# Two 640x640 weight transposes moved from TensorE and piecewise DMA to whole DMA transposes, with exact 128-feature fold chunks, in a gated linear-attention plus GeGLU kernel

## The chip, the cores and the metric

The kernel runs on one core of one Trainium2 chip. The metric is the device time of one execution in microseconds (us). Each kernel was run several times; the medians below are over its runs. Beside the device time, a run reports a *span*: the stretch from the first to the last recorded instruction. The span is some 2 us shorter than the time. The kernel before took 306.58 us (306.54 to 307.19 in four runs).

Names of engines in profile lines: PE is TensorE's matmul side, PEld its weight loads, DVE VectorE, ACT ScalarE, POOL GpSimd, and SPq the sequencer that issues the transfers.

## The reference, cut to what matters

```python
# S = 2048 tokens, D = 640, H = 32 heads of Dh = 20, F = 1728, all bf16
g = sigmoid((x * gate_w).sum(-1, keepdims=True))
q, k, v = split_heads(x @ wqkv)                      # wqkv: 640 x 1920, columns q | k | v
pq = einsum("bhsd,hdf->bhsf", q, w_phi)              # w_phi: one 20x20 matrix per head
pk = einsum("bhsd,hdf->bhsf", k, w_phi)
phi_q = concat([softmax(pq), softmax(-pq)]); phi_k = concat([softmax(pk), softmax(-pk)])
kv = phi_k^T v ;  z = sum_s phi_k                    # per head
o  = (phi_q kv) / (phi_q z + 1e-6)
a  = o @ wo
b  = (gelu(x @ w_gate) * (x @ w_up)) @ w_down
out = g * a + (1 - g) * b
```

Both kernels *fold* w_phi into the projections: x @ Wk @ blockdiag(w_phi) = x @ (Wk @ blockdiag(w_phi)). A fold is a matmul whose stationary operand is a piece of Wk with features on the partitions, that is, Wk *transposed*. So the front of the kernel needs Wk^T and Wq^T (640x640 each), and x^T (features on partitions) for every projection.

## The kernel before: the parts that matter

Everything goes through a helper that waits for the events a buffer needs, then issues. Transfers on the SP queue take 16 semaphore lanes in turn; at the end the SP sequencer waits for each lane and each engine.

```python
def dma(self, qkey, fn, reads=(), writes=(), guard=()):
    q = self.queues[qkey]
    lane = q["rr"]; q["rr"] = (lane + 1) % len(q["lanes"])      # 16 lanes on SP
    ...
def finish(self, eng):
    for q in self.queues.values():
        for L in q["lanes"]:
            if L["count"] > 0: eng.wait_ge(L["sem"], L["count"])
    for e in self.engs.values(): ...                             # then the four engines
```

The loads. k and v come plain, k is transposed on PE later, q is transposed by six DMAs of 640 rows x 128 columns, each starting at a group of six (or four) heads. The transpose of x block 1 is held until the last k/v load has landed, and everything behind it in the queue with it.

```python
xload(0); kvload(0); xload(2)
for kt in range(1, KD): kvload(kt)                    # five loads of 320 KB: k and v
xblock(1, [("wk", KD - 1)])                           # held until the last k/v load landed
for g, (h0, nh) in enumerate(self.GH):                # GH: head groups of 6, 6, 4, 6, 6, 4
    dma_start_transpose(self.wqT[:, g, :], self.wqkv[:, h0*DH : h0*DH + P])
xblock(2); xblock(3)
# ... then the FFN weights
```

PE's front, in order of issue (a fold is six matmuls of 120 or 80 columns):

```python
warm(7); xt(0); xt(1); warm(2)                        # xt: PE transposes of the first x block
vs(0,0); gate_column(3); vs(1,0); xt(2); xt(3)        # vs(t, kt): one step of x_t @ Wv
...                                                   # the rest of vs, the block diagonal
tk(0, 6, "d"); tk(1, 7, "a"); vs(0, 4); ... tk(5, 1, "d")   # 30 PE transposes of k, six copies
fold(0, "k"); fold(1, "k"); v_early(4); fold(2, "k"); ks(0,0); ...; fold(4, "k"); ...
fold(0, "q"); fold(1, "q"); k_early(1); fold(2, "q"); fold(3, "q"); k_early(2); fold(4, "q")
k_early(3); pq(0,1); pq(0,0); pq(0,3); gram(0); pq(0,2)     # pq: an "Eq group", 5 matmuls, 2 exponentials on ACT
```

After that comes a loop over the sixteen token tiles (projection, exponentials, normalisation, Gram matrix) and the FFN. None of it is touched by the change.

The softmax here doesn't subtract the row's maximum and nothing guards it: scores larger than these inputs give would overflow.

## Time and profile before

| | before |
|---|---|
| device time, median | 306.58 us |
| span of the profiled run | 304.5 us |
| PE busy | 296.6 us (97%) |
| first k fold starts | 14.50 us |
| first q fold that waited for DMA | 22.71 us |
| first Eq group starts | 28.23 us |
| third Eq group starts | 30.67 us |

The top of the profile page and its chain summary (share of the span by engine):

```profile
span 304.5 us, 5031 instructions
...
PE 296.6 (97%) x2002; PEld 175.0 (57%) x2028; DVE 162.3 (53%) x317; ACT 105.2 (35%) x186; POOL 30.0 (10%) x61
...
PE 90%; SPq 4%; DMA 3%; ACT 1%; issue 1%; DVE 0%; DVEq 0%; ACTq 0%
```

PE is busy for 97% and is 90% of the chain that ended last; after 50 us its only listed wait is one of 0.2 us.

The list of PE's waits over the whole run (who waited for whom: us in total, times, longest):

```profile
PE ps L532 <- DVE one L528: 1.3, 1, 1.3
PE ps L351 <- DMA wqT<-in_A_wqkv_dram: 0.8, 1, 0.8
PE ps L388 <- DVE w_49 L364: 0.4, 1, 0.4
PE ps L503 <- ACT Eq L509: 0.3, 1, 0.3
...
```

Line 351 is the fold. The first wait is the unavoidable start.

The chain of waits of the first 31 us, in order of time (start, duration, what):

```profile
3.71 5.80 DMA w_49<-in_A_wqkv_dram
...
9.54 2.68 SPq L228
...
12.26 1.26 SPq L233
...
19.28 3.39 DMA wqT<-in_A_wqkv_dram
...
22.71 0.50 PE ps L351 x7
...
24.58 0.58 PE ps L351 x12
...
26.52 0.29 PE ps L351 x6
```

Read it downwards: the k/v loads land at 9.5 us, only then is x block 1 issued (L228), then the q pieces one after another (L233, the first of six shown), and the q folds (L351) start when the last has landed.

The PE timeline shows the folds (start, duration, line and operation, count, idle before):

```profile
11.74 0.72 PE L322 MATMUL ps<-ident,w_49 128*120 128x128 bf16 x10
...
14.50 0.69 PE L351 MATMUL ps<-BD,wkT 120*128 120x120 bf16 x5
...
26.36 0.45 PE L351 MATMUL ps<-BD,wqT 120*128 120x120 bf16 x6
26.65 1.53 PE L371 MATMUL ps<-w_49,xT 128*128 128x384 bf16 x10
28.23 2.10 PE L503 MATMUL ps<-xT,wq_50 128*128 128x512 bf16 x9
30.67 1.25 PE L503 MATMUL ps<-xT,wq_50 128*128 128x512 bf16 x5 [0.34 <-ACT Eq L509]
```

L322 are the PE transposes of k.

### The profile page before, as it was taken

The page shows a single profiled execution, that of the slowest core. Times are in us where ns is not written, and L with a number is a line of the kernel's source. Part 1 is how long each engine was busy: PE and PEld are TensorE (multiplying, and loading weights), DVE is VectorE, ACT ScalarE, POOL GpSimd, SP SyncE. Part 2 cuts the span into 40 slices and gives each one's busy share as a digit, 9 for nine tenths or more (in the row PEclk, how much of TensorE's full clock was granted, in tenths as well). Part 3 has the DMA queues.
Part 4 walks back from the last instruction along what each step waited for, and adds up shares of the span by engine and source line. Part 5 has one row for each costly group of instructions (what it writes and reads, how often), then busy time and mean ns, then how long its engine had stood idle before and what let it go on. Part 6 is the DMA issues. An engine that isn't in the chain of part 4 may idle for free.

```text
span 304.5 us, 5031 instructions
## 1 busy us (share of the span) xinstructions
PE 296.6 (97%) x2002; PEld 175.0 (57%) x2028; DVE 162.3 (53%) x317; ACT 105.2 (35%) x186; POOL 30.0 (10%) x61
## 2 busy tenths in 40 slices
PE   8989999999999999999999999999999999999996
PEld 3656565655555555777545567754457765545763
DVE  1438999986775877234367710435770044567000
ACT  3356776667673222111322211123221122222111
POOL 7200000000000011111011000101110010111000
PEclk9999999999999999999999999999999999999999
DMA  7679994000000011120110111011001001110101
GB/s 242 176 123 248 368 366 156 2 0 0 2 0 2 0 23 25 22 65 23 44 24 0 22 24 43 24 43 23 18 6 43 24 25 43 22 22 2 43 24 43
DMA packets 33043, 18.29 MB, mean 60 GB/s; under 512 B 25147, under 2 KB 32124, under 8 KB 33020
## 3 DMA queue, kind: packets, MB, share of 16 engines
q1 hardware_dynamic: 32368, 17.95, 21.6%
q8 instruction: 16, 0.26, 0.4%
q10 hardware_dynamic: 652, 0.03, 0.1%
q14 instruction: 7, 0.06, 0.1%
HBM read 9.78 MB, written 2.62 MB: 41 GB/s over the span
## 4 chain that ended last, share of the span: by engine, by line
PE 90%; SPq 4%; DMA 3%; ACT 1%; issue 1%; DVE 0%; DVEq 0%; ACTq 0%
PE ps L630 36%; PE ps L712 20%; PE ps L371 11%; PE ps L718 7%; PE ps L503 6%; PE ps L667 4%; PE ps L477 4%; SPq L233 2%; DMA w_49<-in_A_wqkv_dram 2%; PE ps L640 1%; DMA wqT<-in_A_wqkv_dram 1%; SPq L228 1%; SPq L218 1%; ACT Eq L509 1%; PE ps L351 0%
## 5 line engine op out<-in xcount | busy, mean ns | idle before, releaser
L630 PE MATMUL ps<-xT,wu_sb 128*128 128x512 bf16 x253 | 64.2, 379 | 0.8 <-ACT Eq L509 0.2
L712 PE MATMUL ps<-wd_sb,hT 128*128 128x320 bf16 (+2 forms) x447 | 63.5, 299 | 0.1
L630 PE MATMUL ps<-xT,wg_sb 128*128 128x512 bf16 x252 | 63.0, 379 | 0.2
L633 ACT ACTIVATE gl<-ps 128x512 bf16<-128x512 f32 x52 | 31.0, 597 | 83.3 <-PE ps L630 74.2
L635 DVE TENSOR_TENSOR hT<-ps,gl 128x512 bf16<-128x512 f32 x52 | 35.7, 688 | 42.9 <-PE ps L630 42.9
L712 PEld LDWEIGHTS ps<-wd_sb,hT 128*128 128x128 bf16 x448 | 43.1, 98 | 18.2 <-DVE hT L635 0.4
L630 PEld LDWEIGHTS ps<-xT,wu_sb 128*128 128x128 bf16 x260 | 25.4, 98 | 31.1 <-issue 0.7
L630 PEld LDWEIGHTS ps<-xT,wg_sb 128*128 128x128 bf16 x260 | 24.9, 98 | 26.9
L371 PE MATMUL ps<-w_49,xT 128*128 128x512 bf16 (+3 forms) x216 | 39.0, 328 | 0.2
L696 POOL TENSOR_TENSOR Og<-O_57,O_58 128x640 bf16<-128x640 bf16 x16 | 22.3, 1393 | 167.9 <-DVE O_58 L694 167.9
L728 ACT ACTIVATE outsb<-ps,Gm 128x640 bf16<-128x640 f32 (+2 forms) x17 | 13.0, 762 | 74.1 <-PE ps L718 74.1
L371 PEld LDWEIGHTS ps<-w_49,xT 128*128 128x128 bf16 x220 | 20.8, 97 | 18.2
L683 DVE RECIPROCAL RH<-ps 128x32 f32<-128x32 f32 x16 | 5.7, 358 | 43.9 <-PE ps L667 42.8
L449 DVE TENSOR_REDUCE Dk<-Ek 128x64 f32<-128x1280 bf16 x16 | 23.7, 1482 | 7.4 <-ACT gcol L441 7.4
L458 DVE TENSOR_TENSOR Ek<-Ek,Dk 128x640 bf16<-128x640 bf16 x32 | 25.0, 822 | 0.6
L718 PE MATMUL ps<-wo_sb,goT 128*128 128x320 bf16 (+2 forms) x160 | 24.5, 299 | 0.0
L503 PE MATMUL ps<-xT,wq_50 128*128 128x512 bf16 x94 | 23.4, 378 | 0.7 <-ACT Eq L509 0.3
L509 ACT ACTIVATE Eq<-ps 128x512 bf16<-128x512 f32 x40 | 21.8, 607 | 5.8 <-PE ps L503 5.8
L438 ACT ACTIVATE Ek<-ps 128x640 bf16<-128x640 f32 x32 | 20.7, 704 | 4.1 <-PE ps L371 3.1
L718 PEld LDWEIGHTS ps<-wo_sb,goT 128*128 128x128 bf16 x160 | 15.5, 98 | 6.3
L667 PEld LDWEIGHTS ps<-KV,Eq 128*128 128x128 bf16 x192 | 12.0, 98 | 3.1
L667 PE MATMUL ps<-KV,Eq 128*128 128x154 bf16 x192 | 13.7, 221 | 0.0
(73 smaller groups left out, 183.2 us busy)
## 6 DMA issues: line engine op xcount, KB each, us to landing
out_dram<-outsb SPq DMA_DIRECT2D x15, 160.0 KB, 1.8
wd_sb<-in_B_w_down_dram SPq DMA_DIRECT2D x1, 2080.0 KB, 12.6
w_49<-in_A_wqkv_dram SPq DMA_DIRECT2D x5, 320.0 KB, 5.2
wg_sb<-in_B_w_gate_dram SPq DMA_DIRECT2D x1, 1120.0 KB, 6.5
wu_sb<-in_B_w_up_dram SPq DMA_DIRECT2D x1, 1120.0 KB, 9.0
wg_sb<-in_B_w_gate_dram SPq DMA_DIRECT2D x1, 960.0 KB, 8.9
wu_sb<-in_B_w_up_dram SPq DMA_DIRECT2D x1, 960.0 KB, 9.3
wo_sb<-in_A_wo_dram SPq DMA_DIRECT2D x1, 800.0 KB, 10.3
```

The costliest lines, as they stand in the source:

```text
L371: sc.op("pe", lambda e, kt=kt: e.matmul(self.bank(bank)[:, bcol:bcol + n], self.xT[:, kt, t * P:(t + 1) * P], self.w3[:, kt, self.D + c0:s ...
L449: sc.op("dve", lambda e: e.tensor_reduce(self.Dk[:, se, 0, :].rearrange("p (s h) -> p s h", h=H), self.Ek[:, se, :, :].rearrange("p s (h d ...
L458: sc.op("dve", lambda e, v=v, r=r: e.tensor_tensor(v, v, r, ALU.mult), reads=[("Rk", se)], writes=[("Ek", se, s)])
L503: sc.op("pe", lambda e, kt=kt: e.matmul(self.bank(bank), self.wq2[:, kt, i * P:(i + 1) * P], self.xT[:, kt, b * self.BT:(b + 1) * self.BT] ...
L509: sc.op("act", lambda e, s=s, scale=scale: e.activation(self.Eq[:, s, i, b * self.BT:(b + 1) * self.BT], self.bank(bank), AF.Exp, scale=sc ...
L630: sc.op("pe", lambda e, kt=kt, w=w, bk=bk: e.matmul(self.bank(bk), w[:, kt, c * P:(c + 1) * P], xs(kt), start=(kt == 0), stop=(kt == self. ...
L633: sc.op("act", lambda e: e.activation(self.gl[:, slot, :], self.bank(banks[0]), AF.Gelu_apprx_tanh), reads=[("ps", banks[0])], writes=[("g ...
L635: sc.op("dve", lambda e: e.tensor_tensor(self.hT[:, c, :], self.bank(banks[1]), self.gl[:, slot, :], ALU.mult), reads=[("ps", banks[1]), ( ...
L667: sc.op("pe", lambda e, s=s, i=i, n=n, o0=o0, k0=k0, bk=bk, r=r: e.matmul(self.bank(bk)[:, o0:o0 + n], self.Eq[:, s, i, t * P:(t + 1) * P] ...
L696: sc.op("pool", lambda e: e.tensor_tensor(self.Og[:, sl, :], self.O1[:, sl, :], self.O2[:, sl, :], ALU.add), reads=[("O", 0, sl), ("O", 1, ...
L712: sc.op("pe", lambda e: e.matmul(self.bank(bk, w), self.hT[:, c, tt * P:(tt + 1) * P], self.wd_sb[:, c, w0:w0 + w], start=(c == 0), stop=F ...
L718: sc.op("pe", lambda e: e.matmul(self.bank(bk, w), self.goT[:, gs, k, :], self.wo_sb[:, k, w0:w0 + w], start=False, stop=(k == self.KD - 1 ...
```

## The change

Its intent: take the k transposes off PE, take the six q pieces and the held x block off the critical DMA queue, and load x of the first block ahead of the weights. Wk^T and Wq^T each come in one 640x640 DMA transpose. Then their chunks are exact 128-feature chunks, in which heads (20 features) straddle the edges; so the block diagonal is built per chunk with a mask, and folds accumulate overlapping columns in PSUM (six matmuls of 140 or 80 columns instead of 120 or 80).

```diff
@@ loads @@
-        xload(0)
-        kvload(0)
-        xload(2)
-        for kt in range(1, KD):
-            kvload(kt)                     # k and v, 320 KB each
-        xblock(1, [("wk", KD - 1)])
-        for g, (h0, nh) in enumerate(self.GH):
-            sc.dma("sp", ... dma_start_transpose(self.wqT[:, g, :], self.wqkv[:, h0 * DH:h0 * DH + P]) ...)
+        xload(0)
+        xload(2)
+        for kt in range(KD):
+            vload(kt)                      # v alone, 160 KB each
+        def wload(T, c0, key):
+            sc.dma("sp", lambda e: e.dma_start_transpose(T[:, :, :], self.wqkv[:, c0:c0 + D]), writes=[key])
+        wload(self.wkT, D, "wkT")
+        xblock(1)
+        wload(self.wqT, 0, "wqT")
         xblock(2)
         xblock(3)
@@ fold: six matmuls, chunk i of 128 features, heads HLO[i]..HHI[i] @@
+        for i in range(self.KD):
+            lo, hi = self.HLO[i], self.HHI[i]
+            for h in (0, 1):                       # PSUM bank of heads 0-15, 16-31
+                a, z = max(lo, 16 * h), min(hi, 16 * h + 15)
+                ...
+                matmul(bank[:, c0:c0 + n], wT[:, i, kt * P:(kt + 1) * P], self.BD[:, i, k0:k0 + n], start=first, ...)
@@ PE's front @@
-        (two filler matmuls, 30 transposes of k and their copies, k_step(0, kt) between the k folds)
+        f(0, "k", (6, 7), "d")                     # "d": cast on DVE, "a": on ACT
+        f(1, "k", (0, 1), "a")
+        self.v_early(4, 2)
+        f(2, "k", (4, 5), "d")
+        f(3, "k", (6, 7), "d")
+        self.v_early(5, 0)
+        f(4, "k", (4, 5), "d")
+        self.k_early(0, 2)
+        f(0, "q", (6, 7), "d")
+        f(1, "q", (4, 5), "d")
+        self.k_early(1, 0)
+        f(2, "q", (6, 7), "d")
+        f(3, "q", (4, 5), "d")
+        self.k_norm(0)
+        self.k_early(2, 2)
+        f(4, "q", (6, 7), "a")                     # the last cast, now on ACT
+        self.k_norm(1)
+        self.k_early(3, 0)
         self.pq(0, 1, 1)
         self.pq(0, 0, 0)
         self.pq(0, 3, 3)
```

(cut: the order of the x transposes and of the first steps of V, half of V's copies out of PSUM moved from ACT to DVE, the per-chunk block diagonal with the gate column in its second bank, the mask built earlier on POOL, buffer sizes, and keys of the bookkeeping.)

## The prediction

> What bounds the kernel. TensorE: the page has PE busy 296.6 of 304.5 us (97%), and the chain of waits is 90% PE. After 50 us the list of waits shows no PE idle over 0.2 us, so only removing PE work, or PE's gaps in the first 30 us, can pay. The 5 us windows show PE idle 1.3 us in 0–5 (waiting for x), 0.3 in 15–20 and 1.2 in 20–25; "busy" stretches at 14.5–16.1 also hide fold waits. In the chain the 20–25 gap is DMA: x block 1's transpose waits for all five k/v loads (last lands at 9.5 us, a 5.4 us wait of the SP queue), six transposed q pieces then cost 1.27 us of issue each, and the q folds wait for the last until 22.7.
>
> What the change removes.
> - 30 PE transposes of k (timeline: 10 in 0.72, 5 in 0.44; about 65 ns each): about 1.95 us of PE, plus their six copies (0.49 each on DVE, 0.70 on ACT).
> - Two filler matmuls (0.59 us of PE, mostly in a gap that exists anyway).
> - Half of the early plain load: 819 KB of v instead of 1,638 KB of k and v.
> - Fold waits for those copies (about 0.6 us at 14.5–16), the q wait (0.8 us at 22.7), and about 0.5 us before the last k step at 21.2.
>
> What it adds.
> - Two whole 640x640 DMA transposes. Estimate from x blocks (512x640: issue 2.7–2.9 us, landing 4.9–6.6 us after issue, peak near 290 GB/s): issue 3.3 us, data 3 us. The Trainium skill, "DMA: Bandwidth & Descriptors", section "Latency and other measured facts", gives 261 GB/s for non-contiguous and 350–400 for contiguous transposes; this trace's peak lies between. So k^T should land near 10–11 us, x block 1 near 13, q^T near 16, each before its use (12.5, 13.5 and 19).
> - Five block-diagonal matmuls and multiplies instead of two and three: about 0.1 us of PE.
> - A fold stays six matmuls, 720 columns instead of 640. Six took 0.45 us though columns alone need 0.27, so it is weight-load bound: +0.0–0.05 us each.
> - x of both halves before V: V starts at about 6.0 us and runs without gaps for 5.75 us (20 steps of 0.287); folds start at about 12.4 us rather than 14.5.
>
> On the critical path. Following banks and engines by hand: the k folds start 2 us earlier, but lose some to V's evacuations and the last k cast (0.3–0.5 us). The last q fold is now cast on ACT behind three exponentials; the first Eq matmul group needs that bank, a new stall of about 0.5 us. First Eq group: about 26.0 us instead of 28.2; the third (which waited for an Eq evacuation until 30.67) at about 28.7. All later work shifts by that; the FFN doesn't change.
>
> Prediction: 304.6 us, a gain of 2.0 us (0.65%), range 303.4 to 306.2. Faster by over 2%: 0.01; within 2%: 0.97; slower: 0.02.
>
> Right if: the timeline shows the first k fold at 12–13 us, no PE wait for either transposed weight, folds of 0.45–0.5 us, first Eq group near 26 us, PE busy down by about 2 us, and everything after 60 us the same up to a shift.
>
> Wrong if: whole transposes land late (a fold can't start on a piece; if k^T came at 14.5 us the gain would vanish), or transposes, no longer held back, slow the v loads; if new waits around V's evacuations or the last q cast are larger; or if the Eq exponentials on ACT set the pace around 26–31 us. Larger gain if these stalls don't show: up to about 3.3 us.

## The result, and the profile after

| | before | changed |
|---|---|---|
| device time, median | 306.58 us | 303.33 us (302.93 to 303.59, four runs) |
| span of the profiled run | 304.5 us | 301.2 us |
| PE busy | 296.6 us | 294.1 us |
| first k fold starts | 14.50 us | 12.27 us |
| first Eq group starts | 28.23 us | 25.51 us |
| third Eq group starts | 30.67 us | 27.71 us |
| last ACT evacuation ends | 301.97 us | 299.01 us |

The ratio of the fast runs is 0.9888 (95% interval 0.9871 to 0.9905). The gain is 3.25 us by the medians (1.1%), and 3.61 us in the pair of profiled runs (306.54 and 302.93 us).

The page after:

```profile
span 301.2 us, 4951 instructions
...
PE 294.1 (98%) x1973; PEld 173.9 (58%) x1999; DVE 161.4 (54%) x317; ACT 103.5 (34%) x182; POOL 29.0 (10%) x58
...
PE 92%; SPq 2%; DMA 2%; ACT 1%; issue 1%; DVE 0%; DVEq 0%; ACTq 0%
```

PE's waits after, same view:

```profile
...
PE ps L491 <- ACT wq_50 L354: 0.7, 1, 0.7
PE ps L359 <- DMA xT<-in_A_x_dram: 0.6, 1, 0.6
PE ps L359 <- DVE w_49 L352: 0.3, 1, 0.3
...
```

The wait for q is gone. In its place stand a wait for x block 1 and one for the last q cast on ACT.

The chain of waits after, first 29 us:

```profile
4.18 4.09 SPq L226
...
8.31 5.12 DMA xT<-in_A_x_dram
...
13.71 1.31 PE ps L359 x9
15.01 0.63 PE ps L339 x12
...
24.63 0.61 ACT wq_50 L354
...
25.51 1.04 PE ps L491 x4
...
27.71 1.25 PE ps L491 x5
```

L226 is the whole k transpose: issued at 4.18 us, right behind the v loads, and landed 6.3 us later, at 10.5 us. x block 1 landed at 13.4 us. The whole q transpose landed 6.8 us after its issue at 11.26, at about 18.1 us, 0.9 us before its first fold. Two folds (L339, x12) take 0.63 us. The same folds in the PE timeline carry longer durations:

```profile
12.27 0.79 PE L339 MATMUL ps<-BD,wkT 128*128 128x140 bf16 x12
13.71 1.31 PE L359 MATMUL ps<-w_49,xT 128*128 128x512 bf16 x9 [0.65 <-DMA xT<-in_A_x_dram]
...
23.01 0.48 PE L339 MATMUL ps<-BD,wqT 128*128 128x140 bf16 x6
23.32 1.53 PE L359 MATMUL ps<-w_49,xT 128*128 128x384 bf16 x10
25.51 3.46 PE L491 MATMUL ps<-xT,wq_50 128*128 128x512 bf16 x14 [0.66 <-ACT wq_50 L354]
```

Where the time came from, by the traces alone. The third Eq group starts 2.96 us earlier, and from there PE does the same work in the same order: the shift is still 2.96 us at the last ACT evacuation (301.97 less 299.01). So the loop and the FFN gave and took nothing. PE busy fell by 2.57 us between the start of the x transposes and the third Eq group (24.08 to 21.51), and PE idle there by 0.35. The remaining 0.65 us of 3.61 lies *behind* the last evacuation. The packed traces have the spans more exactly than the page, 304.46 and 301.22 us: from the last evacuation to the end of the span it is 2.50 us before and 2.21 after, and from span to device time 2.08 and 1.71.

### The profile page after: what moved, and what is told of

The parts are those of the page before. It is cut to its first block, busy times and chain, and to the rows that moved or that the text cites. A ratio compares the mean times of both kernels' runs of the same rounds, so it can differ in the third digit from the quotient of the medians.

```text
span 301.2 us, 4951 instructions
## 1 busy us (share of the span) xinstructions
PE 294.1 (98%) x1973; PEld 173.9 (58%) x1999; DVE 161.4 (54%) x317; ACT 103.5 (34%) x182; POOL 29.0 (10%) x58
## 4 chain that ended last, share of the span: by engine, by line
PE 92%; SPq 2%; DMA 2%; ACT 1%; issue 1%; DVE 0%; DVEq 0%; ACTq 0%
PE ps L602 36%; PE ps L684 20%; PE ps L359 12%; PE ps L690 7%; PE ps L491 7%; PE ps L639 4%; PE ps L465 4%; DMA xT<-in_A_x_dram 2%; PE ps L612 1%; SPq L226 1%; SPq L216 1%; PE ps L339 1%; ACT Eq L497 1%; ACT Ek L426 0%; DVE w_49 L352 0%
## 5 line engine op out<-in xcount | busy, mean ns | idle before, releaser
L359 PE MATMUL ps<-w_49,xT 128*128 128x512 bf16 (+3 forms) x226 | 40.7, 327 | 1.1 <-DMA xT<-in_A_x_dram 0.6
L359 PEld LDWEIGHTS ps<-w_49,xT 128*128 128x128 bf16 x230 | 21.7, 97 | 19.7 <-DVE w_49 L352 0.7
L491 PEld LDWEIGHTS ps<-xT,wq_50 128*128 128x128 bf16 x100 | 8.6, 97 | 8.8 <-ACT wq_50 L354 0.7
```

The costliest lines, as they stand in the source:

```text
L359: sc.op("pe", lambda e, kt=kt: e.matmul(self.bank(bank)[:, bcol:bcol + n], self.xT[:, kt, t * P:(t + 1) * P], self.w3[:, kt, c0:c0 + n], s ...
L491: sc.op("pe", lambda e, kt=kt: e.matmul(self.bank(bank), self.wq2[:, kt, i * P:(i + 1) * P], self.xT[:, kt, b * self.BT:(b + 1) * self.BT] ...
```

## The experiments

Twelve kernels ran in three calls of four. Each call used one chip, and the kernel before ran beside it: 306.72, 306.65 and 306.43 us. All results were correct. Comparisons with the changed kernel use its rerun as a control, 303.24 us, unless said otherwise; that run shared a chip only with the second call. The start of PE's work varies by some 0.6 us from run to run (the times when x lands), so a profile's PE shift is trusted to a few tenths. Two things blur differences of a few tenths in the device times too. The kernel before was 0.22 us faster on the chip of the third call than on the control's. And the piece between span and device time, about 1.7 us in the changed kernel, is about 2.0 us in some of its variants, for no known cause (point 3 of the explanation); where it matters, spans are given.

Main theory: the gain is the PE work and PE waits taken out of the first 30 us, mostly the k transposes. Rivals: the order of transfers alone did it; the x order did it; a fold costs what the timeline's duration says.

### The control

The unedited changed kernel.

> The changed kernel itself, unedited, as the control on the chip of this batch. Expected 303.0 to 303.6 us.

Measured: 303.24 us (302.85 to 303.64, six runs), ratio to before 0.988. It repeats the result on another chip.

### Only the hold removed from the kernel before

```diff
-        xblock(1, [("wk", KD - 1)])
+        xblock(1)
```

> The kernel before with one edit: the transpose of x block 1, and so the q pieces behind it, no longer waits for the last k/v load. Theory (that hold is what made the q folds wait at 22.7 us): the first q piece is issued at about 7 us instead of 12.3, the q wait of 0.8 us of PE and nothing else goes, so 0.6 to 1.0 us faster than before, leaving about 2.3 us that only the work removed from PE and the waits between its k copies and folds explain. Rival (the change's whole gain is DMA order): 2.5 us or more faster. Rival (the hold protected the k/v loads): the last load lands later, no gain.

Measured: 305.74 us against 306.65, ratio 0.9961 (0.9932 to 0.999), so 0.9 us faster. Its PE timeline has no wait for q left; the first fold of q starts at 21.84 us:

```profile
21.84 0.74 PE L351 MATMUL ps<-BD,wqT 120*128 120x120 bf16 x12
...
30.05 1.25 PE L503 MATMUL ps<-xT,wq 128*128 128x512 bf16 x5 [0.34 <-ACT Eq L509]
```

By the medians of the spans it is 0.75 us (303.85 against 304.6). It follows that the q wait was a real loss, and that it explains at most 0.9 us of 3.25. Transfer order alone is not the gain.

### k back on PE in the changed kernel

k is loaded plain after v, and transposed on PE in five exact chunks; the rest stays.

```diff
-        wload(self.wkT, D, "wkT")
+        for kt in range(KD):
+            sc.dma("sp", lambda e, kt=kt: e.dma_start(self.w3[:, kt, D:2 * D], w3[:, kt, D:2 * D]), writes=[("wk", kt)])
 ... and between the last v steps:
+        self.tk(0, 6, "d"); self.tk(1, 7, "a")     # 5 transposes and a copy each, five times
```

> The changed kernel with one part undone: k is loaded plain after v and transposed on PE in five exact chunks (25 transposes, five copies); whole q transpose, fold layout, x order and schedule stay. Theory (the k transposes are the largest removed term): 25 x 65 ns = 1.6 us of PE comes back, plus up to 0.6 us of waits for the copies, minus the 0.65 us wait for x block 1, whose transpose now starts earlier; net 1.0 to 2.2 us slower than the changed kernel. Rival (the gain is the earlier q and x and the better schedule, the k transposes were hidden in gaps): within 0.5 us of the changed kernel.

Measured: 305.11 us, 1.87 us slower than the changed kernel and still faster than before (ratio 0.9939). Its PE timeline shows a wait for the copies inside the first fold pair:

```profile
13.89 0.53 PE L353 MATMUL ps<-BD,wkT 128*128 128x140 bf16 x5
14.91 0.55 PE L353 MATMUL ps<-BD,wkT 128*128 128x140 bf16 x7 [0.49 <-ACT wkT L338]
```

The first fold starts at 13.89 us against 12.38 in the control, the first Eq group at 27.08 against 25.20: 1.88 us. (By the medians, 0.29 us is the end of the program, which the lane experiment below explains: this kernel has four transfers more. The medians of the spans, 303.1 less 301.3, then leave about 1.5 us.) At 1.5 to 1.9 us the k transposes are the largest single term, as predicted.

### q folds four times over

The six matmuls of q folds 0 to 3 are issued four times; the last pass starts its banks anew, so the result is the same.

```diff
-        for i in range(self.KD):
+        for i in list(range(self.KD)) * (4 if which == "q" and kt < 4 else 1):
```

> The changed kernel with the six matmuls of q folds 0 to 3 issued four times over (72 more matmuls, same result). It measures what one fold costs PE. Theory (a fold occupies PE 0.315 us, as the chain of waits has it, 0.63 for two; the 0.45 to 0.48 us of the timeline includes a pipeline tail under which the next group runs): 12 x 0.315 = 3.8 us slower than the changed kernel. Rival (my prediction's reading, 0.45 us a fold): 5.4 us slower.

Measured: 307.18 us, 3.94 us slower than the changed kernel for twelve more folds: 0.33 us each. In the timeline eight folds start at 19.58 and the next group at 22.10, 0.315 us each, while the group's duration reads 2.68:

```profile
19.58 2.68 PE L339 MATMUL ps<-BD,wqT 128*128 128x140 bf16 x48
22.10 1.52 PE L359 MATMUL ps<-w,xT 128*128 128x384 bf16 x10
```

The reading of 0.45 to 0.5 us a fold, on which the prediction's sum rested, is refuted.

### The last q cast on DVE

```diff
-        self.k_norm(0)
         self.k_early(2, 2)
-        f(4, "q", (6, 7), "a")
+        f(4, "q", (6, 7), "d")
+        self.k_norm(0)
```

> The changed kernel with the last q fold cast on DVE, and the first normalisation behind that cast, so that the first Eq group no longer waits for ACT (0.66 us of PE in the trace). Theory (ACT sets the pace until the third Eq group: three exponentials for tile 3, then two for the first Eq group): first Eq group 0.6 us earlier, third group still at about 27.7 us, total within 0.2 us of the changed kernel. Rival (the listed wait is a real loss): 0.6 us faster.

Measured: 303.0 us, 0.24 us faster than the control, on another chip. The expectation of "within 0.2 us" is just missed, the rival's 0.6 missed by more. The chain of waits shows why only part of it stayed:

```profile
24.91 1.30 ACT Ek L426 x2
...
26.28 0.99 ACT Eq L497 x2
...
27.31 1.25 PE ps L491 x5
```

The first Eq group started at 24.65 us, 0.55 us earlier than in the control, but the third came 2.66 us after it, and PE waited 0.34 us for ACT's Eq exponentials; in the changed kernel the third came 2.20 us after the first. The last evacuation is 0.32 us earlier than in the control (298.60 and 298.92). By the medians of the spans (300.95 and 301.3) the gain is 0.35 us; the device time hides some of it in the piece behind the span, which is 2.0 to 2.1 us in this kernel. So the result lies between the expectation and the rival: the wait for the cast and the wait for ACT's exponentials in part cover one another, and taking the first away uncovers part of the second.

### All transposes held until the v loads have landed

```diff
-        ... self.wqkv[:, c0:c0 + D]), writes=[key])
+        ... self.wqkv[:, c0:c0 + D]), reads=[("wv", KD - 1)] if key == "wkT" else [], writes=[key])
```

> The changed kernel with all transposes held until the last v load has landed, as the kernel before held them for k and v. Theory (the queue of transposes must start right behind the loads, since 17 us of issue stand before the last of them): k transposed lands about 3.5 to 4 us later, near 14 us, PE waits about 2 us at the first fold and again for x block 1 or q; 2 to 3.5 us slower than the changed kernel. Rival (the loads suffer from the early transposes, and holding them helps V): less than 0.5 us slower, with V ending before 12.2 us.

Measured: 309.13 us, 5.9 us slower than the changed kernel, and slower than the kernel before (ratio 1.007). The direction was right, the size far too small. k was issued 3.4 us later (7.6 us instead of 4.2) and landed 2.9 us later, and PE waited 0.9 us for it and 3.5 us for x block 1. And then PE ran at half speed. The windows view of PE (start:end, length, busy, count, granted clock, share and rate of the DMA engines):

```profile
14.30:17.60 3.30, 0.00 (x0) 0.73 1.04 164
17.60:20.00 2.40, 2.32 (x7) 0.50 1.21 273
20.00:22.00 2.00, 2.00 (x19) 0.50 1.17 231
```

The 0.73 of the first line is an average: finer windows show the clock at 1.00 until about 15.8 us, then at 0.50, and back at 1.00 from about 22.6 us. The Trainium skill, "TensorE: Matmul & The Clock Gate", section "What's actually happening", says that PE drops to half rate after an idle window of about 3.4 us and needs such a window of work to recover. This trace agrees with the half rate. The stretches at 0.50, 6.8 us here and 3.4 us in the experiment on pieces, fit a window of that length. But one wait need not itself last 3.4 us before the clock falls: here it fell only 1.6 us into the idle stretch of 3.46 us, before which PE had waited 0.9 us and worked 0.6. The half speed from 17.7 to 22.6 us cost about 2.5 us (an estimate, half of that time), which the expectation did not have. In the profiles of the kernel before and the changed one the clock stays at 1.00, and their longest waits after the start are 0.8 and 0.7 us. One run of the kernel before had a mean clock of 0.994 and took 309.27 us; it was not profiled.

### k and q in pieces

k and q each transposed in five DMAs of 640x128 instead of one.

```diff
-            sc.dma("sp", lambda e: e.dma_start_transpose(T[:, :, :], self.wqkv[:, c0:c0 + D]), writes=[key])
+            for i in range(KD):
+                sc.dma("sp", lambda e, i=i: e.dma_start_transpose(
+                    T[:, i, :], self.wqkv[:, c0 + i * P:c0 + (i + 1) * P]), writes=[(key, i)])
```

> The changed kernel with k and q each transposed in five DMAs of 640x128 instead of one of 640x640, all else equal. Theory (the SP queue's issue is the limit for pieces: 1.27 us each in the kernel before, so 6.4 us for five, against 4.1 and 3.3 us for a whole one): k complete at 13 to 14 us instead of 10.5, x block 1 near 16, q near 22; PE waits 1 to 2 us at the first folds and 2 us at x block 1 or q: 2 to 4 us slower than the changed kernel. Rival (the size of the pieces doesn't matter, only that PE no longer transposes): within 0.5 us.

Measured: 309.28 us, 6.0 us slower than the changed kernel (expected 2 to 4) and slower than before (1.0082, interval 1.0047 to 1.0116). k was complete in time, near 12 us (no wait for it is listed), but its five issues of 1.27 us stood in front of x block 1, which was issued at 10.7 us instead of 8.3:

```profile
PE ps L361 <- DMA xT<-in_A_x_dram: 4.2, 1, 4.2
```

The idle stretch again halved the clock (0.50 from about 17.6 to 21.0 us), which made the loss larger than the wait. So the same change with pieces in the same order loses time: in this order it pays only because k and q come *whole*. Pieces with x block 1 ahead of them were not tried.

### x block 1 first

```diff
-        wload(self.wkT, D, "wkT")
-        xblock(1)
+        xblock(1)
+        wload(self.wkT, D, "wkT")
 ... and v_early(4) before the first k fold, banks moved to suit
```

> The changed kernel with x block 1 transposed before k, and the projection of v for tile 4 before the first folds (banks moved to suit). Theory (PE's wait of 0.65 us for x block 1 at 13.7 us, which also varies from run to run, is a real loss that order alone can remove; k lands at about 13.3 us, just as the first fold wants it): no wait for x, the last k cast still waited for, 0.3 to 0.8 us faster than the changed kernel. Rival (the wait just moves to k or to q, which still lands at about 18.1 us): within 0.2 us.

Measured: 303.76 us, 0.5 us slower than the control on the same chip, with a wider spread (302.85 to 304.71). PE no longer waits for x block 1, but for k (0.28 us), and V ended at 12.77 us in its profile against 12.38, which lies within the variation of the start. Removing one wait by order alone only moved it. The spread is too wide to say more than "no gain".

### x loaded in two halves around the first v block

```diff
         xload(0)
+        vload(0)
         xload(2)
-        for kt in range(KD):
+        for kt in range(1, KD):
             vload(kt)
 ... and two v steps before the second pair of x transposes
```

> The changed kernel with one part undone: the second half of the first x block is loaded behind the first v block again, and two v steps run before its transposes, as in the kernel before. Theory (V only needs to be fed without gaps, and the loads keep ahead of PE either way): V ends within 0.3 us of where it did, 0.0 to 0.4 us slower. Rival (x first is where V's earlier end comes from): 0.6 us or more slower.

Measured: 303.44 us, 0.2 us slower than the control, on another chip; set against the kernel before on each chip, some 0.4 us slower. Its first k fold started at 13.08 us (12.38 in the control), but then x block 1 was no longer waited for, and the first Eq group came at 25.73. The third part of the change's name, x of the first block first, is worth 0.2 to 0.4 us, hardly above the noise.

### The lanes of the final waits

The gain behind the last evacuation needs a cause. In the raw records of the SP sequencer the program ends with a row of waits, each some 61 ns after the one before. A wait that comes while the last output transfer is still landing costs nothing; one that stands behind the wait for that transfer comes after its landing. In the kernel before nine waits follow the landing, in the changed kernel five. The changed kernel issues 54 SP transfers instead of 58, so its last output falls on lane 5 of 16 instead of lane 9. (The compiled row does not run from lane 0 up: most of its twelve records hold two waits, lane 9 stands in the third record and lane 5 in the seventh.) The experiment shifts the lanes of the changed kernel by four and nothing else.

```diff
-            self.queues[q] = {"lanes": lanes, "rr": 0, "eng": eng}
+            self.queues[q] = {"lanes": lanes, "rr": 4 if q == "sp" else 0, "eng": eng}
```

> The changed kernel with nothing moved but the semaphore lane that the first SP transfer takes (lane 4 of 16 instead of 0), so that the last output transfer ends on lane 9, as in the kernel before, instead of lane 5. Theory (part of the gain is an accident of the end: the final waits run over the lanes in order, about 61 ns each, and those behind the last transfer's lane or freed by it come after its landing; the kernel before had nine behind it, the changed kernel five): the end from the last ACT evacuation to the end of the span grows from 2.18 to 2.45-2.5 us, everything before it unchanged: 0.25 to 0.3 us of span slower, and perhaps 0.3 us more outside the span. Rival (the end belongs to something else): end unchanged at 2.18 us.

Measured: 303.49 us, 0.25 us slower than the control, on another chip. The ACT timeline of this kernel, with the span in its heading:

```profile
core 0 of [0], span 302.0 us
...
299.17 0.37 ACT L700 ACTIVATE outsb<-ps,Gm 128x128 bf16<-128x128 f32 x1 [0.37 <-PE ps L690]
```

and of the changed kernel:

```profile
core 0 of [0], span 301.2 us
...
298.64 0.37 ACT L700 ACTIVATE outsb<-ps,Gm 128x128 bf16<-128x128 f32 x1 [0.37 <-PE ps L690]
```

The packed traces have the spans as 302.03 and 301.22 us. From the end of that line to the end of the span: 2.50 us with the lanes shifted, as in the kernel before, and 2.21 without. So 0.29 us of the gain is an accident of how many transfers the program issues. The other profiles with this order of waits bear it out: it is 2.49 to 2.50 us where the last output is on lane 9 or 13, both in the third record (no hold, k on PE, pieces), and 2.21 to 2.22 where it is on lane 5. The piece between span and device time did not move (1.72 and 1.71 us), so that part is not the lanes.

### The front reordered

The three waits that the changed kernel has left are attacked together: the third k fold before the projection of v for tile 4, the fourth and fifth before that of tile 5; the fourth q fold cast on ACT in a gap there, the fifth on DVE inside the first normalisation; the first Gram group between the second and third Eq group.

```diff
         f(1, "k", (0, 1), "a")
+        f(2, "k", (4, 5), "d")
         self.v_early(4, 2)
-        f(2, "k", (4, 5), "d")
         f(3, "k", (6, 7), "d")
+        f(4, "k", (4, 5), "d")
         self.v_early(5, 0)
-        f(4, "k", (4, 5), "d")
...
-        f(3, "q", (4, 5), "d")
-        self.k_norm(0)
+        f(3, "q", (4, 5), "a")
         self.k_early(2, 2)
-        f(4, "q", (6, 7), "a")
+        self.k_norm(0, lambda: f(4, "q", (6, 7), "d"))   # after its reduction
...
         self.pq(0, 0, 0)
-        self.pq(0, 3, 3)
         self.gram(0)
+        self.pq(0, 3, 3)
```

> The changed kernel with its front reordered: third k fold before the projection of v of tile 4, the fourth and fifth before that of tile 5; fourth q fold cast on ACT, fifth on DVE inside the first normalisation; the first Gram group before the third Eq group. Theory (the remaining PE waits, 0.2 to 0.65 us for x block 1, 0.34 for the last k cast and 0.4 to 0.7 for the last q cast, are real and independent): those three waits go, third-group-plus-Gram ends about 0.9 us earlier, 0.6 to 1.2 us faster than the changed kernel. Rival (they are given back at ACT or at q's landing near 18.1 us): within 0.3 us.

Measured: 301.53 us (301.25 to 302.15), ratio to before 0.9844 (0.9827 to 0.9862), 1.7 us faster than the control on another chip. That is more than expected. All of PE's waits that are left:

```profile
PE ps L522 <- DVE one L518: 1.3, 1, 1.3
PE ps L603 <- ACT Eq L499: 0.2, 1, 0.2
PE ps L339 <- ACT vaug L392: 0.2, 1, 0.2
```

The last evacuation of the profiled run ends at 297.74 us, 1.2 us before the control's, and the two profiled runs differ by 1.2 us too (302.85 and 301.67). The control's profiled run was the fastest of its six, and the kernel before was 0.22 us faster on this chip, so the other 0.5 us of the difference between the medians is mostly spread of runs and chips. Moving the Gram group gives PE something to do while ACT exponentiates, which is what the DVE cast alone lacked.

### The front reordered, final waits in order of use

The same, with the engines waited for first and the SP lanes in the order in which they were last used.

```diff
-        for q in self.queues.values():
-            for L in q["lanes"]:
+        (the four engines first)
+        for q in (self.queues["act"], self.queues["pool"], self.queues["sp"]):
+            n = len(q["lanes"])
+            for L in [q["lanes"][(q["rr"] + i) % n] for i in range(n)]:
```

> The reordered kernel with the final waits put in order of use, engines first and the last output transfer's lane last, so that nothing is left to wait for after its landing. Theory: the end from the last ACT evacuation to the end of the span shrinks from 2.18 to about 1.95 us (four or five waits of 61 ns), so 0.2 to 0.3 us faster than the reordered kernel, and 0.8 to 1.5 us faster than the changed one. Rival (these waits are free): no difference.

Measured: 301.52 us, ratio to before 0.984 (0.9825 to 0.9855): no difference from the reordered kernel in time. In the profiles the end did shrink as expected, from 2.22 to 2.00 us (spans of 299.95 and 299.77 us), but the profiled run waited 0.6 us for x block 1, and the medians of four runs, which spread over 0.9 us in the reordered kernel, do not show it. This is the fastest kernel, on a par with the one above it.

## Why the prediction was right or wrong

The mechanism was right, the size was not: a gain of 2.0 us was predicted, 3.25 us was measured, and 303.33 us lies just below the range's lower end of 303.4. The prediction's aside of a gain "up to about 3.3 us" comes near by luck: its condition was that the stalls don't show, and they did, 1.65 us of them (0.65 for x block 1, 0.34 for the last k cast, 0.66 for the last q cast). Point by point:

| step of the prediction | predicted | found |
|---|---|---|
| V runs without gaps, first k fold | 12.4 us | 12.27 us |
| k^T lands | 10-11 us | 10.5 us |
| x block 1 lands | near 13 us | 13.4 us, and waited for: 0.65 us |
| q^T lands | near 16 us | about 18.1 us, still in time for 19.0 |
| PE busy down | about 2 us | 2.5 us (296.6 to 294.1) |
| cost of a fold | 0.45-0.5 us | 0.315 us |
| first Eq group | about 26.0 us | 25.51 us |
| third Eq group | about 28.7 us | 27.71 us |
| all after it | a mere shift | a mere shift (2.96 us), up to the last evacuation |
| the end of the program | not considered | 0.65 us shorter in the profiled pair |

What failed, in the prediction's words:

1. *"Six took 0.45 us though columns alone need 0.27, so it is weight-load bound"*. This was the mis-sized term. 0.45 us is the duration of the group in the timeline, with the tail of the last matmul; 0.27 us is what 640 columns take at the pace of the chain of waits (five matmuls of 512 columns in 1.08 us); PE moves on after 0.29 us, as the chain of waits of the kernel before already said (0.29 for x6, 0.58 for x12). The fourfold q folds measured 0.33 us from the time and 0.315 from the starts. The columns set the pace, not the weight loads: 0.29 us for 640 columns before, 0.315 for 720 after. The Trainium skill, "TensorE: Matmul & The Clock Gate", section "Back-to-back issue gap", has N/2.4 + 2.5 ns from start to start for N columns (for isolated matmuls, as the page puts it); an estimate from it for 4 x 140 and 2 x 80 columns is 315 ns, which this trace hits. Ten folds were thus overcharged by about 1.35 us (10 times 0.45 less 0.315). That the prediction did use it can be worked out: from its first fold at 12.4 us, six projections of 1.37 us, ten folds of 0.45 us and its stalls of 0.4 and 0.5 us lead to its 26.0 us. Not all of it came out, since the shorter folds ran into the waits for x block 1 and the last k cast; at the first Eq group the prediction was 0.5 us too late.

2. *"the third (which waited for an Eq evacuation until 30.67) at about 28.7"*. The wait for the last cast did appear, with 0.66 us. But the sum added to it a further 0.5 us of waiting for ACT's exponentials. The third group came 2.20 us after the first, not 2.7. The DVE cast shows how the two belong together: without the cast's wait, the third came 2.66 us after the first. They are one wait of one engine, ACT, and were counted twice. This is the other 0.5 us.

3. *"All later work shifts by that"*. True to the last evacuation. Behind it, 0.29 us of the profiled pair's difference is in the final waits, and the lane experiment shows all of it as an accident of the number of transfers. The last 0.37 us lies between span and device time. It stays open: this piece was 2.04 to 2.15 us (with spans rounded to 0.1 us) in the runs of the kernel before, 1.67 to 1.77 in all but one of the changed kernel's ten, and back at 2.0 to 2.2 in the kernels with the DVE cast, the pieces and x block 1 first. Nothing tried here orders these values, and no record covers that piece.

The parts together: about 1.0 us for points 1 and 2 (28.7 less 27.71), and 0.65 us for point 3, carry the predicted 2.0 to the profiled pair's 3.6.

What was right: that the gain of the work itself is confined to the first 30 us; that the k transposes are its largest term (1.5 to 1.9 us when undone); that the q wait of 0.8 us was a real loss (0.75 to 0.9 us when the hold alone is removed); that the whole transposes of k and q would land before their use. One of the warnings, that a late transpose would make the gain vanish, was shown by two kernels: held or cut in pieces, the change loses time against the kernel before.

## What to carry to other kernels

Take the cost of a group of matmuls from the start of one group to the start of the next, or from the chain of waits, never from a duration that includes the tail; when counting waits along a critical path, put those that the same engine causes on one time line, so that each is counted once. Put a transpose that must be early into one large DMA right behind the loads it follows, since on a queue of ordered transfers the issue time of small pieces falls on whatever stands behind them. When the last few tenths of a microsecond matter, look at the program's end too: the order of its final waits and the number of its transfers can shift it without any change to the work.

## What the Trainium skill lacked or had wrong

- "TensorE: Matmul & The Clock Gate", section "Back-to-back issue gap", says that in a stream of weight-load and matmul pairs the spacing is about 81 ns at 128 columns and about 131 ns at 512, and that N/2.4 + 2.5 ns holds for isolated gaps. Here, in such streams, six pairs of 140 and 80 columns took 315 ns (52.5 ns each on average), and fourteen pairs of 128 columns near the end of the kernel before 0.78 us from the start of the group to the start of the next (300.34 to 301.12 us, 56 ns each), and groups of five of 512 columns 1.08 us in the chain of waits (216 ns each): the simple formula holds, and the other two figures do not.
- "DMA: Bandwidth & Descriptors", section "Latency and other measured facts", has rates of DMA transposes but not what their issue costs the queue, and the page's counts of cycles per transpose instruction are for other sizes. Measured: 1.27 us for 640x128 (1.7 to 2.1 for some), 2.7 to 3.6 us for most of 512x640 and up to 5.7 us right behind plain loads, 3.3 to 4.1 us for 640x640 in the changed kernel, with landings 6.3 to 6.8 us after issue. A row of small pieces, issued one after another, so went no faster than 164 KB in 1.27 us, 129 GB/s.
- No page has the cost of a row of waits that are already satisfied ("Advanced Engine Details and Errata" comes nearest, with the time to read one semaphore): the SP sequencer's final waits follow each other at about 61 ns, and four of them more behind the last transfer's landing went with an end 0.29 us longer.
- No page says what lies between the span of the profile and the device time, 1.7 to 2.2 us here, which differed by some 0.3 us between kernels for no cause found; "Runtime: NRT & Kernel Launch" lists steps around a kernel, but no run here shows which of them fall into it.
- "TensorE: Matmul & The Clock Gate", section "What's actually happening", has the half rate after an idle window of about 3.4 us. The half rate was confirmed at waits of 3.5 and 4.2 us (granted clock 0.50, for 6.8 and 3.4 us), but it began 1.6 us into the first wait, and 0.4 us after the end of the second: the length of one wait alone does not tell when.
